# Folding a long convolution's transforms by reflection, and summing a gated unit in the output by DMA

## The chip, the core and the metric

The kernel runs on one core of a Trainium2 chip. The core has five engines that work side by side, each through its own queue in order: TensorE (PE; its weight loads are shown as PEld), VectorE (DVE), ScalarE (ACT), GpSimd (POOL) and SyncE (SP). Data comes and goes by 16 DMA engines, whose transfers are issued from SP's and POOL's queues. PE writes its results to PSUM (eight banks of 128 partitions by 512 float32 each), from where DVE or ACT move them to SBUF.

The metric is the time on the device in microseconds (us). Lower is better.

## What is computed

The input `x` is 2048 rows of 512 channels. Two results are mixed by a gate of each row:

```python
g = sigmoid((x * gate_w).sum(-1, keepdims=True))
# a: a long convolution of each channel; its kernel comes from 128 complex states
K[d, l] = real(sum_n C[d, n] * exp(dt[d] * A[d, n] * l) * dt[d] * B[d, n])
a = irfft(rfft(pad(x.T)) * rfft(pad(K)))[..., :2048].T + x * Dskip
# b: a gated unit, 512 -> 1792 -> 512
b = (sigmoid(x @ w_gate) * (x @ w_up)) @ w_down
out = g * a + (1 - g) * b
```

All inputs and the output are float32.

## The kernel before

**Dense work (b).** The rows are taken in two halves of 1024, each in two blocks of 512 columns (`sb`); the 1792 hidden channels in 14 slices of 128. Each operand of a dense product is split into a high part that PE's fast float32 mode takes whole and a low rest (ACT copies the high part, line 884; DVE subtracts, 885), and a product is three matmuls. `hidden` (938) makes one slice of gate and up for one block: four turns of PE of six matmuls (line 953). `post` (991) applies the sigmoid, multiplies and splits the result. `down` (1013) multiplies with `w_down` in groups of 3, 4, 4 and 3 slices, three matmuls per turn (1030). `add` (1040) scales a group's sum by 1 - g: the first group goes to an accumulator in SBUF (1046), the next ones through a staging tile `part` (1053) and an accumulating DMA from POOL into it (1055); for the second half's last group DVE adds from PSUM (1066). The first half's sums go out to a DRAM tile `acc0` (1060). The split weights of the first half's 14 slices are stored in DRAM (`wsp`, from `keep`, 932) and loaded again for the second half (913 and the next function).

**The convolution's kernel (a).** Channels come in 16 groups of 32. For each group `bases` (408) makes angles, sines, cosines and powers; `tables` (491) builds a table T of 32 steps by five doublings (`double`, lines 459 to 461, DVE), `magnitudes` (465) a table B of 64 (ACT's exponentials, DVE's products, 471 to 486). One batch of 128 small matmuls, `kps` (527), multiplies T with B to the group's kernel of 2048 samples. `first` (536) sorts it (541), adds Dskip, does the first step of its transform (`wps`, 555) and brings it out (`kev`, 565) to a DRAM tile `a_k`.

**The transforms.** The long transform is done in two steps with DRAM between them. `rows` (581) loads 16 tiles of 128 rows of x, takes the dot product with `gate_w` (591) and does u's first step (`ups`, 606), stored in `a_u`. `passes` (633) then works on two halves of the channels (j = 0, 1; 256 each), each in eight parts p: `ustep` (677; `s2u`, 690) is u's second step, `kstep` (702; `s2k`, 715) the kernel's, with the complex product on DVE (726 to 733); `inverse` (738; `ips`, 761) is the first step back, brought out by `evict` (769) to `b_s`. When all eight parts are there, `finals` (795) loads `b_s` again and `last` (810) does the last step (`fps`, 819) and adds g times it to the sums (828 for the first half, which is loaded from and stored to DRAM, 835 for the second).

**The order.** Every generator above yields its steps with the engine that runs them. The order of all steps is written out by hand in the string ORDER: each letter names a kind and an engine ("hidden PE", "tables DVE", "add POOL"), one turn each, and `Plan.run` (202) takes the steps in that order. So the sequence on each engine's queue is fixed by ORDER, and the turns ahead of any step can be counted in it; a turn is one step as it is yielded, which may hold several instructions. "-" turns only take buffers. The PSUM banks are three for `hidden`, one for `down` (joined with the others at the end), four for the rest.

Matmuls come in tile modes: dense work uses the whole 128x128 array, the batches use it as several smaller arrays side by side: kps 128x32 (rows by columns), wps and ips 32x64, ups 64x128, s2u and s2k 64x32, fps 128x64.

Of the kernel before, what the change touches and what calls it, by code (L numbers as in the profile page):

```python
# [32 lines left out]
L, D, F, NS = 2048, 512, 1792, 128  # L33
# [6 lines left out]
ANGLES = list(range(33)) + [64 << k for k in range(5)]  # L40
NA = len(ANGLES)
POWERS = list(range(1, 64, 2)) + ANGLES[33:]
NP = len(POWERS)
# [3 lines left out]
WIDTHS = [256, 256]  # L47
BANKS = dict(gu=3, dn=1, xb=4)
# [3 lines left out]
TURNS = ("ustep PE", "ustep ACT", "ustep DVE", "ustep -", "inv PE", "inv ACT", "inv DVE", "inv SP", "inv -", "x SP", "w SP",  # L52
         "split ACT", "split DVE", "rows PE", "rows ACT", "rows DVE", "rows SP", "rows -", "dn SP", "urest ACT", "urest DVE",
         "urest SP", "bases ACT", "bases DVE", "bases -", "tables PE", "tables DVE", "tables -", "first PE", "first ACT", "first DVE",
         "first SP", "first -", "mags ACT", "mags DVE", "hidden PE", "post ACT", "post DVE", "down PE", "add ACT", "add DVE",
         "add SP", "add POOL", "passes SP", "step PE", "step DVE", "step -", "finals SP", "last PE", "last DVE", "last SP", "last -",
         "const SP", "steps DVE", "steps SP", "preludes ACT", "preludes DVE", "preludes SP", "pw SP", "splitw ACT", "splitw DVE",
         "splitw SP", "splitd ACT", "splitd DVE", "splitd SP")
ORDER = (
    "211JLMK78jJLK7MJLK8jjMj1j07JLMjjK78jjJLSkKj2K!8jjJJ77#lkL8jjMlkmS!L55MS#!8jjJ643M4X0RLMkXYlWXjjkjjkWQPOjllRNWlkmlWj#9UKW"  # L60
    "jKmXj78TWaikaanR7hahaaa$Ql9maaPiiiikmjlKSXXam7ORNRQP0$TjjnVjmVmK75!Tjkm8akYjWXlOnRNWjmjTkjljUkamWm0jal9aRQaWP8ORN#RQPnaV"
    "blVUOZ9WXKTRNV8WaiaaaaVKkRjaaQmaadeTVhmhTmaPlijnkig7Vj7iiORcdmjddmNKRlXXkmTYjKjQTPjWaaXnVmkjjOaaV7WRkmlWlWW5mNaa8lnk8XWT"
    "b8Zla$ijV7Taa8kjaajjjaalaaRQPhhjimiidORN$de9miaKXaS!a9#VkljmKVTTSgSjXn!VcY#jWX7dkkjdmjR7KjkmVladdQPORjNRWQPOlfaWakabZlU8"
    "RWlNWjX!#VWdaik8jlTjahmahmnaaj43eTmkm7mmg0ajajiTjaiicRinmmKQP8ORq7ljk4madmXjdXYWk$jjdadVnqlmmaXWNRQPkOWaWm8aaaVTmWqan9lX"
    "KTW7VbZRNlVaidTT9ahjh$qaaKaakmmaajm8jegRQPkajikiiOmna7ciXmaqXdmVdm5majYWXanVmmmaRlldWaWVajmWlqKb8WjX7kNWUlZ9aijja8kVajK7"
    "ajaRnQaaqhjhljka9Paadmmk8dK7m$mnORNRTQijljjiiilS!Xj#Sk5XSYWTkPK!ejX!7l#Tmmaja#amWaf9jklalgcORjabWS!WklK#VVkdjZWdlm7XWdNK"
    "djdnmmm8qjmRaihhqTTkaaaaeQagcdnjmm7mmd8qaajdPiiiiXXaYW$nqj89K7jOakXWWWWaamRmaamamalVlNnXW8bZaKkkih$am8jjjmlm43qamaVhT4ji"
    "iTaadfni7mmmmkjinmmmmaXaaXYqW8jXdenWagaacjqamjqJSaalkdjabm5W!#SWWlX!#ldZVj$mLjWJVkakmdddiheVghScaaanlLajkldMj9admjimJidj"
    "jkiiaX!#dmjXYaaW$XnamjmLWJqW9mljanmWaaWKVaLjkaabMZMXfrrrrrrkqdllmmMeWaKpnJai5DABBusrrtktrJgalatjhjjammlJhicddddqijatjraI"
    "EjqakrkimFaJilFDFKFXLlHnXABMBusYkjWttXLmtatLmWrrajlrkaWajIjMHEFFrrrmjnmmW$WLmDABarBaGGHqSpuabHsplnprrXkZWtmlmamiajkardeg"  # L70
    "ttljcMnMmmhhratIraajadSiiaid$jddEFiFamDrFAFBXHBustHtXYkWtaqtjkXrjInajjEaGljkqWFWrFalFlrDABWrkrmaBaabmjustSlWXfmnrZWmtmjm"
    "jdHaihtj4eKaarqg3tkancr4mamhiiadiIdaiadaXmnjkrlKjrmaHdEFrFFFKaXmYaDmnHHAlWkBBaXuWsrajarrlabmjkpWWtlrmttjmrnkZtplrjWXjdIE"
    "rGDmWaipFaeFFaHHABBusrrrrrtjatahtathiii$mimjkaagncajXjdammdXYIddEFFFFaKDmWjkqaXSABHpBusljrjtjaHWtttInmmkEaaGabjkWfFljFFW"
    "ZWXlWjkSaiajdajHaheghlaamcaHvladjkkiajvdvzwyivzwyiSvvlxjyxldidkaXyXjkYzyjlnmmvaWXSjaWjjklWaWjaWjxaabvlXmZwyyzxKyklvvWaai"
    "wyjvjykldhxmnjmzhiimmmaxikqvniyXljmazakwwmxmxxxyaXjYmyWaXvjyvxnmamxWekammgncWmaldWaaajdaWmzaamXjdbwldZxWKxmnjjdmkmmaiham"
    "KaaafhaajneamgacdKaakamivqjaidddmviajmizawabxZnmmdxSSllekgcdddjdjfrrrrljkljkljkjjjjmkjlrjrDrlrrrrkACBuKsttttklDjrjlqkrjq"
    "SArBrBustjmjnmljktqSktrtIErrrrrrFFGrGGlmqjDlFklFmHFjjmqqHnACBursrrDrmrmtttmmntqACCHuHstjjtmtmtIKmmnrEGDmrrFrrrFFHrDmmmrj"
    "kljFFKACCuFFHsrjnrkmHtrlmmyttABBtustttmjktnmIjmEFjmGFHDFFqFGmnrABrGCuslrkttmttrrmrmrrmnDjHHABCustmtHtrjtHmmljqSIEklFFGjk"
    "mGSjGjkGGjSFlyHnmmlklmjjkqjomHHmlHmovvzvvwyzwyxvjjvzyxmjmyvyvzvmjyvzkwywkxqyvvzvwlxxxjqyyvyzljyjmkvlmvmzykmmxylxwxkwwylm"
    "mmxoxoqxyypxoqxmopmmpxpmommxmoypp")  # L80

XLATE = 0
SLACK = dict(dma=1.6, eng=0.06)
FETCH = 6.5


def constants():
# [7 lines left out]
    wf = fwd.reshape(P, 64) / L  # L95
    wk = np.tile(fwd.reshape(P, 2, 32).transpose(2, 1, 0).reshape(32, 2 * P), (4, 1))
    l2, k2 = np.arange(32)[:, None], np.arange(32)[None, :]
    wwu = np.zeros((8, 2, 32, 2, 4, 2, 32))
    wwv = np.zeros((8, 4, 32, 2, 2, 32, 2))
    for p in range(8):  # L100
        for r in range(2):
# [1040 lines left out]
```

## Time and profile before

| | |
|---|---|
| runs | 619.85, 624.1 and 628.68 us, median 624.1 us |
| profiled execution | span of 621.9 us, from the first instruction to the last; it is one execution, and no time of its own beside the span is recorded |
| busy | PE 609.1, DVE 518.1, ACT 426.5, POOL 35.1 us |
| granted clock of TensorE | 0.997 of full on the mean |
| DMA | 140.35 MB, mean 226 GB/s |
| instructions | 16371 |

The profile is one execution. A row of a group of instructions has the line in the kernel, the engine, the operation, the tiles written and read, the shapes, the count, then busy time in us and the mean length of one in ns, and last the idle time of the engine ahead of them with what ended it. Lengths of successive instructions overlap a little. A row of the timeline has start, length, engine, line and count. A chain row is a stretch of the chain of work that ended last, followed back from the end. SPq is SP's queue of DMA issues.

### The profile page before, as it was taken

To read this page: it belongs to the slowest core of one execution; us is meant where nothing else is said; L and a number is where in the kernel's file an instruction comes from. 1 tells how busy PE (TensorE), PEld (TensorE's weight loads), DVE (VectorE), ACT (ScalarE), POOL (GpSimd) and SP (SyncE) were. 2 spreads that over 40 slices of the span, in tenths; PEclk is the share of its full clock that TensorE was granted. 3 is DMA by queue.
4 is the path that set the end of the run, shared out by engine and by line. 5 is a ranking of instruction groups with operands and counts; after the bars stand their busy time and mean duration, and the time that the engine had idled before them with its cause. 6 is when DMAs were issued, how large, how long until landed. Compare 5 with 4: busy or idle time off the path is not lost.

```text
span 621.9 us, 16371 instructions
## 1 busy us (share of the span) xinstructions
PE 609.1 (98%) x6816; PEld 462.3 (74%) x6816; DVE 518.1 (83%) x927; ACT 426.5 (69%) x705; POOL 35.1 (6%) x44
## 2 busy tenths in 40 slices
PE   6999999999999999999999999999999999999997
PEld 4877777777778777877767777777787777667775
DVE  5879999998999999999999999997996276438334
ACT  6698897979899988998878787768585221322110
POOL 0000000011110101010100000000110001100000
PEclk9999999999999999999999999999999999989999
DMA  6964775594595729899999869666775989999784
GB/s 220 373 220 131 218 270 172 172 292 115 175 358 177 203 36 298 293 295 271 200 289 288 245 154 274 197 192 223 224 207 155 253 206 240 236 269 257 212 269 146
DMA packets 97162, 140.35 MB, mean 226 GB/s; under 512 B 40000, under 2 KB 65472, under 8 KB 92480
## 3 DMA queue, kind: packets, MB, share of 16 engines
q1 hardware_dynamic: 91328, 128.81, 67.7%
q0 software_dynamic: 5760, 10.49, 10.2%
q8 instruction: 54, 0.88, 0.6%
q14 instruction: 20, 0.16, 0.1%
HBM read 75.31 MB, written 53.48 MB: 207 GB/s over the span
## 4 chain that ended last, share of the span: by engine, by line
PE 84%; DVE 6%; DMA 4%; ACT 4%; issue 1%; SPq 1%; DVEq 0%
PE gups L953 44%; PE dps L1030 22%; PE kps L527 4%; PE ups L606 3%; PE wps L555 3%; PE fps L819 2%; PE ips L761 2%; PE s2u L690 2%; PE s2k L715 2%; DMA ak<-a_k 1%; DMA gu<-wsp 1%; DMA a_k<-kev 1%; DVE T L460 1%; DMA st<-wgu 1%; DVE uf L727 1%
## 5 line engine op out<-in xcount | busy, mean ns | idle before, releaser
L953 PE MATMUL gups<-x,gu 128*128 128x512 f32 x1344 | 334.0, 396 | 6.1 <-ACT gu L884 6.1
L953 PEld LDWEIGHTS gups<-x,gu 128*128 128x128 f32 x1344 | 251.0, 189 | 74.2 <-issue 13.4
L1030 PE MATMUL dps<-dnw,h 128*128 128x512 f32 x672 | 177.2, 397 | 0.3 <-issue 0.3
L1030 PEld LDWEIGHTS dps<-dnw,h 128*128 128x128 f32 x672 | 123.8, 188 | 36.2 <-issue 9.2
L1055 POOL DMA_DIRECT2D acc<-part x40 | 34.9, 873 | 542.4 <-ACT part L1053 510.9
L1001 ACT ACTIVATE h<-sg 128x512 fp32r<-128x512 f32 x56 | 34.7, 627 | 30.5 <-DVE sg L997 30.3
L477 ACT ACTIVATE B<-B 128x32 f32<-128x32 f32 (+2 forms) x96 | 53.3, 668 | 0.4
L997 DVE TENSOR_TENSOR sg<-gups,sg 128x512 f32<-128x512 f32 x56 | 38.2, 685 | 17.6 <-PE gups L953 13.3
L1053 ACT ACTIVATE part<-dps,omg 128x512 f32<-128x512 f32 x40 | 27.4, 686 | 31.1 <-PE dps L1030 30.8
L461 DVE TENSOR_TENSOR T<-T,t 128x64 f32<-128x64 f32 (+4 forms) x80 | 46.5, 582 | 1.3
L459 DVE TENSOR_TENSOR t<-T,bz 128x64 f32<-128x64 f32 (+4 forms) x80 | 46.2, 577 | 1.1
L460 DVE TENSOR_TENSOR T<-T,bz 128x64 f32<-128x64 f32 (+4 forms) x80 | 46.3, 579 | 0.0
L995 ACT ACTIVATE sg<-gups 128x512 f32<-128x512 f32 x56 | 33.4, 596 | 15.2 <-PE gups L953 15.0
L1002 DVE TENSOR_TENSOR h<-sg,h 128x512 fp32r<-128x512 f32 x56 | 38.2, 686 | 5.7 <-ACT h L1001 5.7
L565 ACT ACTIVATE kev<-wps 128x256 f32<-128x256 f32 x64 | 34.7, 643 | 7.0 <-PE wps L555 6.9
L527 PEld LDWEIGHTS kps<-B,T 128*32 128x32 f32 x2048 | 29.3, 110 | 8.3 <-issue 4.5
L527 PE MATMUL kps<-B,T 128*32 128x64 f32 x2048 | 31.9, 220 | 0.5 <-DVE T L461 0.5
L297 ACT ACTIVATE ev<-ips 128x256 f32<-128x256 f32 x47 | 14.6, 390 | 25.5 <-PE ips L761 25.5
L297 ACT ACTIVATE uf<-s2u 128x512 f32<-128x512 f32 x24 | 13.4, 596 | 24.1 <-PE s2u L690 23.9
L726 DVE TENSOR_TENSOR tt<-s2k,uf 128x512 f32<-128x512 f32 x32 | 22.0, 686 | 4.1 <-PE s2k L715 3.9
L434 ACT ACTIVATE af<-ex 128x1216 f32<-128x1216 f32 x16 | 19.6, 1222 | 7.5 <-DVE ex L431 7.5
L995 ACT ACT_TABLE_LOAD x19 | 24.4, 1283 | 0.3
(87 smaller groups left out, 700.5 us busy)
## 6 DMA issues: line engine op xcount, KB each, us to landing
wsp<-gu SPq DMA_DIRECT2D x14, 1024.0 KB, 6.6
gu<-wsp SPq DMA_DIRECT2D x14, 1024.0 KB, 7.4
acc<-part POOLq DMA_DIRECT2D x40, 256.0 KB, 5.9
a_u<-evu SPq DMA_DIRECT2D x32, 256.0 KB, 4.9
a_k<-kev SPq DMA_DIRECT2D x8, 1024.0 KB, 5.6
au<-a_u SPq DMA_DIRECT2D x32, 256.0 KB, 5.3
ak<-a_k SPq DMA_DIRECT2D x32, 256.0 KB, 6.8
b_s<-ev SPq DMA_DIRECT2D x32, 256.0 KB, 4.4
```

The source lines that it names most:

```text
L459: yield "DVE", dve(n), lambda: V.tensor_tensor(t2, src, sb, op=OP.mult), [t, slot.t]
L460: t = yield "DVE", dve(n), lambda: V.tensor_tensor(dst, src, br, op=OP.mult), [t]
L461: t = yield "DVE", dve(n), lambda: V.tensor_tensor(dst, dst, t2[:, :, ::-1], op=OP.add), [t]
L477: A.activation(B[:, :, 0, 1 << k::2 << k], B[:, :, 0, 1:64 >> k:2], AF.Exp, scale=float(1 << k))
L527: mm(p[32 * jj:32 * jj + 32, s], T[:, ch, c], B[:, ch, c], start=(c == 0), stop=(c == 1), tile_position=(0, 32 * jj), skip_group_check=True)
L565: te = yield "ACT", 0.475, lambda: A.activation(kev[:, :, o:o + 2].rearrange("p k s -> p s k"), ph[jj], AF.Copy), [t, kv.t]
L953: mm(p, gu[:, a, k, dc], x[:, b, dc], start=(dc + n == 0), stop=(dc == NC - 1 and n == 2))
L995: t = yield "ACT", ("sig", act(512)), lambda: A.activation(sg, pg_, AF.Sigmoid), [tg, ss.t]
L997: t = yield "DVE", dve(512), lambda: V.tensor_tensor(sg, pu, sg, op=OP.mult), [t, tu]
L1002: t = yield "DVE", dve(512), lambda: V.tensor_tensor(h[:, 1], sg, h[:, 0].bitcast(F32), op=OP.subtract), [t]
L1030: mm(p, h[:, a, 128 * s:128 * s + 128], dn[:, b], start=(f == f0 and n == 0), stop=(f == f0 + gn - 1 and n == 2))
L1055: ts = yield "POOL", kb(430), lambda: nc.gpsimd.dma_start(accs[t], part, accum_op=OP.add), [te, begun[t]]
```

## The change

- **Folding.** The rows of x are laid out so that each sample stands across from its mirror images. `rows` works on four blocks of four tiles: DVE forms sums and differences of mirrored tiles (two folds of two instructions with 1024 elements each), and u's first step needs then half of the products: 8 batches `ups` of 16 matmuls in 32x32 tiles instead of 16 batches. `ustep` does two parts p at once in 8 batches of 32 matmuls in 32x32 tiles; `inverse` likewise; `last` makes folded sums for four tiles at once (8 batches), which DVE unfolds (four instructions of 512), ACT scales by g.
- **Sums in the output.** There are no accumulators in SBUF any more, and no `acc0`. The first group's scaled sum is written to the output by SP; all others, and the convolution's part (`last`), are added to the output in DRAM by accumulating DMAs from POOL: 48 of 256 KB and 32 of 128 KB instead of 40 of 256 KB into SBUF.
- **Second half in reverse.** The second half takes the slices of the hidden channels from the last to the first; the last three slices' split weights stay in SBUF, and 11 instead of 14 are stored and loaded again.
- **Tables by pairs.** T is built for 64 channels at once (the last doubling in two parts); angles stay per group (32 instead of 38 of them), the powers are made per pair of groups. `wps` takes two groups per batch and is brought out by two ACT instructions of 1024 elements instead of eight of 256.
- **Banks.** The four banks of the batches become two pairs; `kps` takes `down`'s bank.
- **Order.** ORDER is written anew for these steps.

```diff
-ANGLES = list(range(33)) + [64 << k for k in range(5)]
+ANGLES = [b + 0.5 for b in range(32)]
+SCALES = [31.5] + [64 << k for k in range(5)]
-BANKS = dict(gu=3, dn=1, xb=4)
+BANKS = dict(gu=3, dn=1, xb=2)
...
+    XB = slots(ps, "xb", BANKS["xb"], [P, 2, 512])
...
+    def double(T, b, e, parts, t):
+        nd = 64 // parts
+        n = 2 * nd * e
+        for i in range(parts):
...
+            yield "DVE", dve(n), lambda: V.tensor_tensor(t2, src, sb, op=OP.mult), [t, slot.t]
+            te = yield "DVE", dve(n), lambda: V.tensor_tensor(dst, src, br, op=OP.mult), [t]
+            te = yield "DVE", dve(n), lambda: V.tensor_tensor(dst, dst, t2[:, :, ::-1], op=OP.add), [te]
...
+                t = yield from double(T, bz[:, :, k], e, max(1, e // 8), t)
...
+                bank, = yield DNS, 1
+                p = bank.tile("kps", [P, 8, 64])
...
+            def fold(a, b):
+                V.tensor_tensor(a, a, b, op=OP.add)
+                V.scalar_tensor_tensor(b, b, -2.0, a, op0=OP.mult, op1=OP.add)
+            t = yield "DVE", 2 * dve(1024) + 0.2, lambda: fold(u[:, 0], u[:, 1]), tu
+            t = yield "DVE", 2 * dve(1024) + 0.2, lambda: fold(u[:, :, 0], u[:, :, 1]), [t]
...
+                                mm(ph[jj // 2][o:o + 32, jj % 2], wu[rr, c, r], u[rr, c, e], start=True, stop=True,
+                                   tile_position=(32 * jj, o), skip_group_check=True)
...
+                            mm(pu[s][32 * g_:32 * g_ + 32, r, i], wwu[q, i, g_], au[i][q, g_], start=True, stop=True,
+                               tile_position=(64 * s + 32 * r, 32 * g_), skip_group_check=True)
...
+                            mm(pi[g_ // 2][o:o + 32, g_ % 2, i], wwv[q, i, r], uf[q, i, r, c], start=True, stop=True,
+                               tile_position=(32 * g_, o), skip_group_check=True)
...
+        def sums():
+            V.tensor_tensor(mn[:, 0], ph[:, 0], yt, op=OP.add)
+            V.tensor_tensor(mn[:, 1], ph[:, 0], yt, op=OP.subtract)
...
+                t1.append((yield "ACT", act(W) + 0.1, lambda: A.activation(y[:, i], y[:, i], AF.Copy, scale=g[:, t:t + 1]), [te]))
...
+                done.append((yield "POOL", kb(215), lambda: nc.gpsimd.dma_start(out[t, :, cols], y[:, i], accum_op=OP.add), [max(t1), begun[t]]))
...
-        ("sg", 3, [P, 512], F32), ("hs", 8, [P, 2, 512], F32R), ("acc", 8, [P, D], F32)))
+        ("sg", 3, [P, 512], F32), ("hs", 8, [P, 2, 512], F32R)))
...
+    KEEP = GROUPS[-1]
+    SLICES = [list(range(NF)), list(range(NF - 1, -1, -1))]
...
+        te = yield "ACT", act(512) + 0.1, lambda: A.activation(part, p, AF.Copy, scale=omg[:, t:t + 1]), [tp, gate[t, 1].t, ss.t]
+        bank.free(te)
+        if gi == 0:
+            ts = yield "SP", kb(256), lambda: S.dma_start(out[t], part), [te]
+        else:
+            ts = yield "POOL", kb(430), lambda: nc.gpsimd.dma_start(out[t], part, accum_op=OP.add), [te, begun[t]]
```

More of the change, by code (lines that the diff above doesn't have):

```diff
@@ L612, in urest @@
+    def urest(t4, e, i, ph, banks, tp):
         es, = yield EVU, 1
         ev = es.tile("evu")
[L614 to L621 removed]
@@ L685, in mms, with kstep @@
+    def kstep(i, wks, wwk, sk, ak, ready, both, tk):
+        yield ready[0]
+        ufs, uf = ready[1]
+        yield near(tk)
+        bank, = yield XB, 1
+        pk = bank.tile("s2k", [P, 2, 2, W])
         def mms():
@@ L693, in ustep @@
-        sa.free(t)
-        tu = 0.0
-        for r in range(2):
-            te = yield ("ACT", "DVE"), {"ACT": act(2 * w), "DVE": dve(2 * w)}, lambda eng: copy(eng, uf[:, r], pu[r]), [t, ufs.t]
-            banks[r].free(te)
-            tu = max(tu, te)
-        ready[1] = ufs, uf, tu
-        ready[0].set(tu)
-    def kstep(j, wus, wwu, sk, ak, ready, both, tk):
-        w = WIDTHS[j]
-        yield ready[0]
-        ufs, uf, tu = ready[1]
-        yield near(tk)
+        t = yield "PE", ("64x32", 0.92, 66), mms, [tk, bank.t]
```

1009 lines of the change are left out of this document (517 added, 492 removed).

## The prediction

> **What bounds the kernel now.** I read the page's first part and its chain of waits, then the busy time of the engines in five stretches (cut at the eleventh and the last table batch), then single rows.
>
> ```profile
> PE 609.1 (98%) x6816; PEld 462.3 (74%) x6816; DVE 518.1 (83%) x927; ACT 426.5 (69%) x705; POOL 35.1 (6%) x44
> ...
> PE 84%; DVE 6%; DMA 4%; ACT 4%; issue 1%; SPq 1%; DVEq 0%
> ```
>
> TensorE is busy nearly all the time and carries 84% of the chain. Read alone, that says: whatever is taken off PE is gained. The stretches say more (columns: length, busy time of PE, PEld, DVE, ACT, POOL, each with its instructions, granted clock, DMA share, GB/s):
>
> ```profile
> 0.00:40.00 40.00, 33.89 (x136) 26.30 (x137) 28.56 (x71) 27.54 (x42) 0.20 (x4) 1.00 0.77 266
> 40.00:340.00 300.00, 299.51 (x3442) 227.41 (x3441) 289.26 (x499) 267.34 (x439) 21.00 (x24) 1.00 0.77 225
> 340.00:474.00 134.00, 133.53 (x1768) 102.24 (x1767) 124.70 (x221) 98.57 (x158) 5.20 (x6) 1.00 0.71 211
> 474.00:560.00 86.00, 84.30 (x1086) 62.74 (x1084) 43.67 (x80) 23.71 (x50) 6.64 (x8) 0.98 0.98 237
> 560.00:622.00 62.00, 57.86 (x399) 43.65 (x390) 31.86 (x59) 9.31 (x18) 2.08 (x3) 1.00 0.74 221
> ```
>
> Up to the last table batch (474) there are two full engines: PE, and VectorE with 442.5 of 474 us. Only behind it is DVE half idle, and there DMA is full for 86 us (0.98). The eleventh table batch shows how the two meet:
>
> ```profile
> 338.60 1.22 DVE L461 TENSOR_TENSOR T<-T,t 128x1024 f32<-128x1024 f32 x1
> ...
> 339.99 1.21 PE L527 MATMUL kps<-B,T 128*32 128x64 f32 x72
> ```
>
> DVE's last table product ends at 339.82, and PE starts the batch 0.17 us later. Both queues are in order and written out in ORDER, so a new order can be judged at each table turn by two sums: the PE work ahead of it, and the DVE work that its table needs.
>
> **What the change takes off PE.** The prices of PE's work (start and length of runs on the chain; then rows of the timeline, where a batch is charged from its start to that of the next row):
>
> ```profile
> 39.52 1.36 PE dps L1030 x6
> ...
> 64.51 1.92 PE kps L527 x128
> ...
> 106.18 1.14 PE wps L555 x63
> ...
> 508.52 1.91 PE ips L761 x64
> ...
> 587.98 1.88 PE fps L819 x16
> ```
> ```profile
> 323.30 1.09 PE L690 MATMUL s2u<-au,wwu 64*32 64x256 f32 x32
> 324.19 1.67 PE L715 MATMUL s2k<-ak,wwu 64*32 64x256 f32 x32
> ...
> 331.46 1.12 PE L761 MATMUL ips<-uf,wwv 32*64 32x256 f32 x32
> 332.51 1.66 PE L953 MATMUL gups<-x,gu 128*128 128x512 f32 x6
> ...
> 338.07 1.09 PE L715 MATMUL s2k<-ak,wwu 64*32 64x256 f32 x32
> 339.10 0.96 PE L1030 MATMUL dps<-dnw,h 128*128 128x512 f32 x3
> ```
> ```profile
> 32.71 1.13 PE L606 MATMUL ups<-u,wu 64*128 64x512 f32 x4
> 33.77 0.96 PE L1030 MATMUL dps<-dnw,h 128*128 128x512 f32 x3
> ```
>
> A hidden turn (6 dense matmuls) is 1.36, a down turn (3) 0.68; s2u 0.89 (s2k follows it in the same tile mode), s2k 1.03, ips 1.05 (a double one 1.91), ups 1.06, fps 0.94 (two in 1.88), kps 1.92, wps 1.14. Dense work and kps stay. Folding halves the batches of ups, s2u and fps (16 each to 8 each) and brings ips from eight single and four double ones to 8; wps pairs its batches (16 to 8 double ones). The new batches of ups, s2u and ips use 32x32 tiles, which no row shows. Between the nearest rows: 16 tiles that run together need what a half-sized grid needs for half the work, 1.0; if only eight ran together, 1.91, as the double ips. I take 1.05, nearest to ips, which already uses four row strips; wps double 2.05, fps 1.0. Saved: ups 17.0-8.4 = 8.6, s2u 14.2-8.4 = 5.8, ips 16.0-8.4 = 7.6, fps 15.0-8.0 = 7.0, wps 18.2-16.4 = 1.8: 30.8 us. Changes of tile mode (adjacent PE turns of different mode in ORDER) fall from 158 to 133, some 0.1 each (s2k, followed by another mode, costs 0.14 more than s2u): 2.5. So PE's queue, start of 6.1, turns times prices and changes, shrinks from 606.6 (its measured end is 617.9, below) to 573.2.
>
> **What it does to DVE.** The rows that price it, by form:
>
> ```profile
> L421 DVE TENSOR_TENSOR ex<-pp,pw 128x1216 f32<-128x1216 f32 x16 | 22.7, 1419 | 0.1
> ...
> L486 DVE TENSOR_TENSOR B<-B,ex 128x1024 f32<-128x1024 f32 x16 | 19.5, 1219 | 0.0
> ...
> L443 DVE TENSOR_TENSOR bz<-ex,ep 128x320 f32<-128x320 f32 x16 | 12.5, 783 | 7.0 <-ACT ep L438 6.8
> ...
> L459 DVE TENSOR_TENSOR t<-T,bz 128x512 f32<-128x512 f32 x16 | 11.0, 687 | 0.1
> ...
> L541 ACT ACTIVATE kst<-kps 128x512 f32<-128x512 f32 x16 | 9.5, 593 | 2.3 <-PE kps L527 2.3
> ...
> L459 DVE TENSOR_TENSOR t<-T,bz 128x256 f32<-128x256 f32 x16 | 6.7, 421 | 0.2
> ...
> L423 DVE TENSOR_TENSOR ep<-pp,pw 128x160 f32<-128x160 f32 x16 | 5.1, 318 | 0.0
> ...
> L459 DVE TENSOR_TENSOR t<-T,bz 128x128 f32<-128x128 f32 x16 | 4.7, 291 | 0.3
> ```
> ```profile
> 254.54 0.69 DVE L1002 TENSOR_TENSOR h<-sg,h 128x512 fp32r<-128x512 f32 x1
> 255.14 0.29 DVE L459 TENSOR_TENSOR t<-T,bz 128x128 f32<-128x128 f32 x1
> ```
>
> Back to back, an instruction costs some 0.085 us less than its row (0.60 between starts for 0.69). So 1024 elements cost 1.135, 512 cost 0.60, 256 cost 0.335. Ahead of the eleventh table turn, old order against new, counted along ORDER:
>
> Folds of u: 16 instructions of 1024, new, +18.2. Products of the passes: nine pairs of 512 and eight of 256 (16.3) against two pairs of 1024 and two of 512 (6.9), -9.4. Tables: 11 groups of 8.05 (15 products and a start) against 6 pairs of 14.35 (18 products and a start), -2.5; pairing saves the fixed part of the small products but the sixth pair must be whole. Angles: 12 groups of 3.60 against 24 products of 1.135 and 6 power sets; the set's 640-element product lies between 0.78 (if the 320-element row is all layout) and 1.57 (twice it), I take 1.4, together 43.2 against 43.1. Hidden results: 65 against 59 of 0.60, -3.6. Evictions and small ones -1.0. Sum +1.6: the folding adds on DVE what the merging saves. DVE was busy 28.56 + 289.26 = 317.8 by then, 12.9 of it stalls between dependent instructions (the same count of rows gives 305); with 451 instead of 554 instructions the stalls lose 2.4. So **DVE needs 317 busy us before the eleventh table, as it did.**
>
> PE's sum ahead of the same turn falls from 334.9 (measured 340.0) to 292.5: 129 hidden and 100 down turns instead of 137 and 115 (the first eight of the hidden ones are half turns), 28 batches instead of 50, 52 mode changes instead of 83. PE will stand and wait for the table. Behind it PE has 280.7: 99 hidden turns 134.6, 124 down turns 84.3, 14 kstep 14.4, six tables 11.5, last 8.0, inv 7.4, ustep 6.3, three second 6.2, changes 8.1. (The old order had 271.7.) Without any stall, DVE's need is 4 to 16 us above PE's sum at every table (308 against 292.5 here, 422 against 418.8 at the last); in the old order it was 12 to 43 below (305 against 334.9, 425 against 467.7).
>
> The Trainium skill says, in "TensorEngine Tiling (Array Packing)", Performance Considerations (PSUM Bottleneck), that tiling speeds TensorE but not the emptying of PSUM, which may become the bound. By that rule PE's saving need not be the time's saving; the trace has DVE full in the same way (289 of 300 us), though more with tables than with emptying.
>
> **The sum.** DVE was idle 11.4 us in the first 40 and 10.7 in the next 300. With PE waiting for DVE, idle time is bounded by 2 (the first load) and 22 (as before); the new order feeds folds and dots of u to DVE in the first 40 us, so I take 9. Table at 317 + 9 = 326. Then 280.7. Later waits were 617.9 - 340.0 - 271.7 = 6.2; bounds 0 and 8, I take 2, since fewer weight reloads meet the full DMA. The end:
>
> ```profile
> 615.65 2.20 PE L1030 MATMUL dps<-dnw,h 128*128 128x512 f32 x9
> ...
> 617.89 0.75 DVE L1066 SCALAR_TENSOR_TENSOR acc<-dps,omg,acc 128x512 f32<-128x512 f32 x1 [0.90 <-PE dps L1030]
> ```
> ```profile
> acc<-part POOLq DMA_DIRECT2D x40, 256.0 KB, 5.9
> ...
> out<-acc SPq DMA_DIRECT2D x8, 256.0 KB, 2.2
> ```
>
> PE ended at 617.9, and DVE's 0.75 and a store of 2.2 brought 621.9. Now the tail is an ACT scaling and an accumulating DMA of 5.9 instead of 2.2: 4.0 + 3.7, and up to three issues queued ahead on POOL, 7 to 11; I take 7. Sum 326 + 280.7 + 2 + 7 = 616 for the span. The median of the runs (624.1) stands 2.2 above the profiled span (621.9), which gives **618**.
>
> At nothing I cost: ACT (ahead of that turn 6% less work by the same count; the merged kev evictions replace the old ones); the weights of three slices that stay in SBUF instead of going out and back (13.6 MB with the sums' store and reload; PE stood still for 1 us in all between 40 and 474, at DMA shares of 0.77 and 0.71); the sums' own traffic (24 more accumulations' worth against the loads saved); SP's issues. Behind 474 DVE gets 28 us of sums of folded rows, but was idle 72.5 of 148 there. If DMA's relief counts, it takes the later waits to 0; if not, they are 6 to 8. Two waits are new on PE. kps now shares the single bank of down, which is free again after ACT's 0.593 copy; behind every table turn ORDER has a hidden turn or another batch (1.03 or more) before the next down turn, so nothing; without that cover 16 x 0.7 = 11. And a batch of ups, s2u, ips or wps now takes both bank pairs, each emptied by a copy of 1024 (1.2); 63 of the 72 batches follow dense work, the other nine could stand 1.1 each, 10 in all, at least 0; 1 of my 2 us is for that.
>
> **Rivals.** (1) PE stays the bound: 573.2 + 11.3 (measured minus counted, 617.9 - 606.6) + 7 = 592, on the runs 594. For it: 98% and 84%. Against: it needs the eleventh table at 298 (292.5 and the old order's 5.1 of waits), while DVE has 317 busy us of work before; the count would have to be 20 us too high. (2) The accumulating queue at the end: rows 8 to 15 get their last group and their second final sum within PE's last 30 us, all on POOL in order, and each second one must wait until the first has landed (5.9); behind it stand the other accumulations, with them the staging tiles that ACT's scaling needs (six instead of eight), and so PSUM banks. If all eight pairs wait in full, 47 us stand in 30, with other issues behind them, and the last landings come 17 to 20 late: 638, slower. It decides where a pair lies closer than 6 us; in ORDER two pairs do (3 to 5 us of PE work apart), the others are 7 to 10 apart, so I give it little. "DMA: Bandwidth & Descriptors", Rules for kernel authors, in the Trainium skill demands that wait for any accumulation beside another access of the same bytes; no run here shows an accumulation in DRAM. (3) 32x32 tiles run only eight at a time: 0.9 more for each of 24 batches; those ahead of the eleventh table hide in PE's wait, the 13 behind add 12: 630.
>
> **Chances.** Forecast 0.66 (own range 605 to 634: idle 2 to 22, waits 0 to 8, tail 7 to 11, not all at an end), (1) 0.14, (2) 0.12, (3) 0.05, others 0.03. A change of 2% (to 611.6 or 636.6) is about what can be told from none. Faster: (1), a quarter of the forecast, and half of the others: 0.32. Slower: half of (2) and a twelfth of the forecast, with scraps: 0.13. Within: 0.55. The range 600 to 637 leaves out (1) and the far part of (2).
>
> **What would show it.** PE's busy share falls from 98% to about 93 to 95%, with waits of the table batches (kps) for DVE's T or B growing from 0.5 us in all to 20 or more, nearly all up to the eleventh table; DVE stays near 97% up to the eleventh table; dense matmuls keep 1.36 for six; a 32x32 batch takes 1.0 to 1.1; the span ends 6 or 7 us behind PE's last matmul. I am wrong if the eleventh table starts before 315 (DVE's count too high), if PE idles behind it for more than 10 us (DMA or PSUM slots), or if POOL's waits reach the end.

## The result, and the profile after

| | before | changed |
|---|---|---|
| median of the runs | 623.8 us (619.85 to 628.68, 4 runs) | 657.3 us (653.4 to 659.1, 4 runs) |
| ratio | | 1.053, 95% interval 1.047 to 1.059 |
| profiled span | 621.9 us | 655.8 us |
| start of the eleventh table batch | 340.0 | 334.2 (predicted 326) |
| start of the last table batch | 474.1 | 463.8 |
| PE's last matmul ends | 617.9 | 644.4 |

The changed kernel is slower by 5%; the prediction (618, range 600 to 637) was wrong, and on the wrong side of no change. Up to the last table it is 10 us ahead, and the stage behind it is 44 us longer (192.0 us instead of 147.8). Some of the 44 was planned: counted along ORDER, PE's own work behind the last table grew from 139 to 154 us (534 dense matmuls instead of 450), and by the sum of the forecast that stage should have taken 163 us. So 28 to 29 us of it are lost. Two of the four executions of e3 (676.4 and 678.7 us) and of e4 (659.9 and 660.0) took over 1.5% longer than the fastest of their kernel; times and ratios below leave them out, but the only profile of e4 is of the one of 660.0. The page of the changed kernel: busy times, the granted clock and the DMA share in 40 slices, the chain of waits by engine.

```profile
PE 599.2 (91%) x7136; PEld 454.4 (69%) x7136; DVE 518.2 (79%) x726; ACT 444.3 (68%) x668; POOL 70.3 (11%) x84
...
PEclk9799989999999999997999999999899989999997
DMA  7585581668828686964389469186599999999988
...
PE 45%; DVE 17%; issue 12%; DMA 11%; ACT 6%; SPq 4%; POOL 4%; POOLq 0%; DVEq 0%; ACTq 0%
```

PE carried 84% of the chain and now carries 45%; no engine has taken its place, the rest is spread over DVE, DMA, waits and issues. The last 11 slices of the DMA row lie behind the last table: nothing but nines and eights. The stretches, cut at the eleventh and the last table batch (columns as in the prediction: length, busy time of PE, PEld, DVE, ACT, POOL, granted clock, DMA share, GB/s):

```profile
0.00:40.00 40.00, 28.36 (x149) 18.68 (x149) 32.63 (x79) 23.68 (x41) 0.20 (x4) 0.91 0.73 236
40.00:334.20 294.20, 275.37 (x3337) 216.09 (x3340) 285.50 (x389) 256.65 (x376) 17.55 (x20) 0.98 0.64 184
334.20:463.80 129.60, 128.47 (x1846) 99.88 (x1844) 119.36 (x153) 104.14 (x150) 5.21 (x6) 1.00 0.69 193
463.80:560.00 96.20, 86.77 (x1102) 62.56 (x1109) 45.19 (x60) 29.57 (x50) 17.87 (x21) 0.95 1.00 244
560.00:620.00 60.00, 56.75 (x572) 39.97 (x566) 25.58 (x34) 19.47 (x35) 11.11 (x13) 1.00 1.08 267
620.00:656.00 36.00, 23.49 (x154) 17.27 (x152) 9.97 (x15) 10.76 (x20) 18.36 (x21) 0.89 0.89 120
```

Up to the eleventh table DVE was busy 32.63 + 285.50 = 318.1 us, and idle for 16. Behind the last table DVE and ACT are idle for more than half of the time (busy 80.7 and 59.8 of 192), PE is not full either (167.0 of 192), and the DMA share is 0.9 to 1.1 to the end. Single rows of its timeline, by stage:

```profile
27.17 1.14 PE L661 MATMUL ups<-u,wu 32*32 32x512 f32 x32
28.24 8.45 PE L1040 MATMUL gups<-x,gu 128*128 128x512 f32 x36
...
334.16 1.04 PE L577 MATMUL kps<-B,T 128*32 128x64 f32 x60
...
366.77 1.49 PE L823 MATMUL ips<-uf,wwv 32*32 32x256 f32 x64
368.20 3.01 PE L1040 MATMUL gups<-x,gu 128*128 128x512 f32 x12
...
377.94 1.49 PE L761 MATMUL s2u<-au,wwu 32*32 32x256 f32 x64
379.36 4.37 PE L1040 MATMUL gups<-x,gu 128*128 128x512 f32 x18
...
463.78 1.88 PE L577 MATMUL kps<-B,T 128*32 128x64 f32 x119
469.62 0.33 PE L577 MATMUL kps<-B,T 128*32 128x64 f32 x9 [3.97 <-issue]
...
637.55 6.87 PE L1110 MATMUL dps<-dnw,h 128*128 128x512 f32 x29 [0.23 <-DVE h L1088]
...
649.31 0.87 POOL L1129 DMA_DIRECT2D out<-part  x1 [0.42 <-issue]
```

A batch of ups takes 1.07 as predicted, but ips and s2u take 1.43 and 1.42 instead of 1.05 (the trace has two instructions for each of the program's matmuls in these batches, 32 for ups and 64 for the others). The last table batch stands still in its middle for 3.97 us. Behind PE's end POOL still issues accumulations up to 649.3 and the last ones land near the span's end.

The forecast span was 616; measured 655.8. By the steps of its sum: the eleventh table 334.2 instead of 326, +8.2; from there to PE's end 310.2 instead of 280.7 + 2, +27.5 (3.4 of it ahead of the last table); the tail 11.4 instead of 7, +4.4.

What PE waited for up to the eleventh table, and then what DVE, ACT and PE waited for behind the last one (time in all, times, longest):

```profile
PE kps L577 <- DVE B L515: 8.1, 3, 3.3
PE gups L1040 <- ACT gu L946: 6.3, 1, 6.3
PE gups L1040 <- DVE x L947: 4.6, 2, 2.3
PE gups L1040 <- ACT sg L1081: 3.8, 3, 1.9
```
```profile
DVE ev L309 <- DMA out<-mn: 9.2, 1, 9.2
...
ACT ev L309 <- DMA out<-mn: 6.1, 2, 4.1
...
DVE yt L309 <- DMA out<-yt: 4.6, 1, 4.6
...
PE s2k L788 <- DVE ev L309: 3.2, 1, 3.2
```

The 6.3 us are the start, which the kernel before has too (6.1). For the rest of the front ACT stands among PE's releasers as often as DVE, seven times each, for 9.1 us against 14.0. Behind, the evictions of `ips` (tile `ev`) and the unfolding (`yt`) stand for accumulations of the final sums (`mn`, `yt`) to land: those tiles share two tags with the passes and are held until POOL's accumulating DMA is done. PE then waits for the evictions. And the DMA queues behind the last table, before and after (packets, MB, the packets' time as a share of 16 engines over that stage of 147.8 and 192.0 us; q0 is POOL's queue, q1 SP's):

```profile
q1 hardware_dynamic: 34256, 31.20, 76.3%
q0 software_dynamic: 1440, 2.62, 11.0%
```
```profile
q1 hardware_dynamic: 35480, 33.59, 64.4%
q0 software_dynamic: 7776, 9.96, 35.2%
```

In time: 112.8 + 16.3 = 129 of 147.8 us before, 123.6 + 67.6 = 191 of 192.0 after. SP's queue moved about as much as before; the accumulations went from 2.6 to 10.0 MB, and a MB of them took 6.8 us, where SP's took 3.7. This gave three theories for the 28 us (of the 40) that are lost behind the last table, the tail with them. *Order*: accumulations into the same row wait for each other, in POOL's order. *Slots*: tiles held until an accumulation lands. *Traffic*: the DMA engines are full, and the accumulations are what fills them. And one for the front: *ring*, DVE and ACT bound it together.

### The profile page after: what moved, and what is told of

Read it like the earlier page. It is cut to its first block, busy times and chain, and to the rows that moved or that the text cites. A ratio compares the mean times of both kernels' runs of the same rounds, so it can differ in the third digit from the quotient of the medians.

```text
span 655.8 us, 16738 instructions
## 1 busy us (share of the span) xinstructions
PE 599.2 (91%) x7136; PEld 454.4 (69%) x7136; DVE 518.2 (79%) x726; ACT 444.3 (68%) x668; POOL 70.3 (11%) x84
## 3 DMA queue, kind: packets, MB, share of 16 engines
HBM read 67.97 MB, written 63.44 MB: 200 GB/s over the span
## 4 chain that ended last, share of the span: by engine, by line
PE 45%; DVE 17%; issue 12%; DMA 11%; ACT 6%; SPq 4%; POOL 4%; POOLq 0%; DVEq 0%; ACTq 0%
PE gups L1040 23%; PE dps L1110 11%; PE kps L577 4%; POOL out L905 3%; PE wps L607 2%; PE s2k L788 2%; DMA out<-mn 2%; DMA u<-xp 2%; DMA ak<-a_k 1%; DMA out<-part 1%; DMA out<-yt 1%; DVE t L533 1%; DVE sg L1083 1%; DVE T L535 1%; DVE T L534 1%
## 5 line engine op out<-in xcount | busy, mean ns | idle before, releaser
L1129 POOL DMA_DIRECT2D out<-part x48 | 42.6, 888 | 482.9 <-ACT part L1124 337.3
L1124 ACT ACTIVATE part<-dps,omg 128x512 f32<-128x512 f32 x64 | 43.6, 681 | 63.7 <-PE dps L1110 60.9
L1087 ACT ACTIVATE h<-sg 128x512 fp32r<-128x512 f32 x56 | 34.9, 626 | 16.5 <-DVE sg L1083 16.2
L533 DVE TENSOR_TENSOR t<-T,bz 128x1024 f32<-128x1024 f32 (+3 forms) x48 | 41.3, 861 | 1.5 <-ACT ez L436 0.9
L535 DVE TENSOR_TENSOR T<-T,t 128x1024 f32<-128x1024 f32 (+3 forms) x48 | 41.4, 863 | 0.2
L534 DVE TENSOR_TENSOR T<-T,bz 128x1024 f32<-128x1024 f32 (+3 forms) x48 | 41.5, 864 | 0.0
L616 ACT ACTIVATE kev<-wps 128x1024 f32<-128x1024 f32 x16 | 31.0, 2006 | 5.5 <-PE wps L607 5.5
L798 DVE TENSOR_TENSOR tt<-s2k,uf 128x1024 f32<-128x1024 f32 x16 | 19.6, 1225 | 18.4 <-PE s2k L788 18.3
L431 ACT ACTIVATE af<-ex 128x1024 int32<-128x1024 f32 x16 | 16.9, 1059 | 13.3 <-DVE ex L484 13.3
L788 PE MATMUL s2k<-ak,wwk 64*32 64x256 f32 x512 | 19.2, 397 | 5.7 <-DVE ev L309 3.2
L901 ACT ACTIVATE yt<-yt,g 128x256 f32<-128x256 f32 x16 | 7.4, 502 | 24.7 <-DVE yt L894 24.7
```

Source lines behind the costliest of these rows:

```text
L533: yield "DVE", dve(n), lambda: V.tensor_tensor(t2, src, sb, op=OP.mult), [t, slot.t]
L534: te = yield "DVE", dve(n), lambda: V.tensor_tensor(dst, src, br, op=OP.mult), [t]
L535: te = yield "DVE", dve(n), lambda: V.tensor_tensor(dst, dst, t2[:, :, ::-1], op=OP.add), [te]
L1087: t = yield "ACT", act(512), lambda: A.activation(h[:, 0], sg, AF.Copy), [t, hs.t]
L1124: te = yield "ACT", act(512) + 0.1, lambda: A.activation(part, p, AF.Copy, scale=omg[:, t:t + 1]), [tp, gate[t, 1].t, ss.t]
L1129: ts = yield "POOL", kb(430), lambda: nc.gpsimd.dma_start(out[t], part, accum_op=OP.add), [te, begun[t]]
```

## Experiments behind the last table

**Final sums as plain stores, final sums into their own rows, final sums from their own tiles.**

```diff
-nc.gpsimd.dma_start(out[t, :, cols], y[:, i], accum_op=OP.add)
+nc.gpsimd.dma_start(fsc[t, :, cols], y[:, i])                    # e1
+nc.gpsimd.dma_start(b_s[j][i, int(slot is es), 4 * t4:4 * t4 + 2]
+    .rearrange("j k d -> (j k) d"), y[:, i], accum_op=OP.add)    # e2
```
```diff
-        ts, = yield fin["t"], 1
-        es, = yield fin["ev"], 1
+        ts, = yield EZ, 1
+        es, = yield KST, 1                                       # e3
```

> The 32 final sums (128 KB each) go as plain stores to a scratch array instead of accumulating into the output rows; the convolution's part is left out of the output, every issue stays where it was on POOL. Three theories of the 27.5 us lost behind the eleventh table and of the 4.4 us in the tail. Order (an accumulation waits for the one before it in the same row, and POOL behind it): dense excess behind the last table goes from 16.6 back to some 6, the tail from 11.4 to about 8, so 657 - 11 - 3 = 643. Slots (the finals' tiles lie in the passes' two tags and are held until their accumulations land): the same place, but a plain store still holds them for a landing, so half of it: 650. Traffic (the DMA queues are full from 464 to 620, and an accumulation moves its bytes twice): 4.2 MB less at some 240 GB/s are 17 us: 640. None of these (batch prices, clock, code loading): 656.

> The 32 final sums still accumulate, with the same bytes, from the same tiles, in the same place of POOL's queue, but into rows of the scratch array that fed them, which nothing else touches by then; the convolution's part is left out of the output. Order: no wait for an earlier accumulation of the row, so as without accumulation, 643 (657 - 14). Slots: tiles are held for one landing instead of a wait and a landing, 650. Traffic: nothing is saved, 657.

> Nothing is left out: the finals' two tiles move from the tags that they share with the passes (t, ev) to two tiles of the tables that are free by then (ez, kst), one each. Order: the same accumulations in the same order, 655. Slots: the evictions of ips and the products of s2k no longer wait for an accumulation's landing; of the gaps of PE behind the last table the two at 533 and 565 (3.3 and 2.3) and the dense excess of 16.6 shrink, 657 - 13 = 644. Traffic: 657.

Measured: e1 650.6 us (ratio to the kernel before 1.048, interval 1.043 to 1.054), e2 651.9 (1.050, 1.045 to 1.054), e3 669.7 (1.078, 1.068 to 1.088). Without the waits for the same row, and with all the traffic, e2 is 5 us faster than the changed kernel by the medians, but by the ratios the two can't be told apart (1.050 and 1.053, with overlapping intervals); taking the accumulation out of the final sums (e1) adds hardly anything to that. None of the three gives the 13 to 17 us that its theory promised. e3 went the other way by 12, with a stage behind the last table of 210.4 instead of 192.0, and its timeline says how:

```profile
496.17 0.69 DVE L309 COPY yt<-fps 128x512 f32<-128x512 f32 x1 [9.50 <-DMA out<-yt]
...
502.31 0.69 DVE L888 TENSOR_TENSOR mn<-fps,yt 128x512 f32<-128x512 f32 x1 [5.45 <-DMA out<-mn]
502.92 0.68 DVE L889 TENSOR_TENSOR mn<-fps,yt 128x512 f32<-128x512 f32 x1
...
503.70 2.33 PE L761 MATMUL s2u<-au,wwu 32*32 32x256 f32 x60 [7.71 <-issue]
```

With one own tile each (in the changed kernel behind the last table they have two, shared), every set of final sums waits for the last set's accumulation to land; DVE stands 9.5 and 5.5 us with its queue behind it; the bank of `fps` stays full, and PE stands 7.7 us for it in the middle of a batch (the profile calls that "issue", since the wait is for a bank that DVE gives back at 503.6). So held tiles are a real cost, but the way to lower it is more tiles:

**More tiles.** Behind the last table the two tables of 16 KB are cut up (order of all engines unchanged):

```diff
-                for n, s in (("big", TB[0]), ("big", KEV[0]), ("big", EX[0]), ("uf", TA[0]), ("ev", T2[0]), ("t", T2[1]), ...
+                for src, names in ((TB, ("mn", "mn", "mn", "yt", "yt")), (TA, ("uf", "mn", "yt", "yt")),
+                                   (KEV, ("big", "big")), (EX, ("big", "big"))):
```

> Nothing is left out: behind the last table the two 16 KB tables are cut into pieces, so that the finals have four pairs of tiles of their own and the passes one more load tile than now; order of all engines unchanged. Slots: no eviction and no bank waits for an accumulation's landing: with one own pair instead of shared ones the time rose by 18, with four it falls to what the own rows gave or lower, 645 to 650. Traffic: within 3 of 657. Order (same row): POOL's waits stay, 655.

Measured: 655.0 us, ratio 1.051 (1.044 to 1.059), which cannot be told from the changed kernel's 1.053. The waits of PE for evictions are gone, and others stand in their place:

```profile
PE fps L898 <- DMA b_in<-b_s: 3.6, 4, 1.5
PE s2u L783 <- DMA au<-a_u: 2.2, 1, 2.2
```

The waits have moved from landings of accumulations to landings of loads. That speaks for traffic, which the next three kernels change directly.

**All accumulations plain; and, the other way, more traffic.**

```diff
-nc.gpsimd.dma_start(out[t], part, accum_op=OP.add)
+nc.gpsimd.dma_start(gsc[gi - 1, t], part)          # e5, with the stores of e1
```
```diff
-lambda: S.dma_start(b[q][64 * c:64 * c + 64], src)
+lambda: (S.dma_start(b[q][64 * c:64 * c + 64], src), S.dma_start(xsc[...], src))   # e6; e12 likewise
```

> All accumulations (the 48 group sums of 256 KB and the 32 final sums of 128 KB) go as plain stores to scratch arrays; the output keeps the first group's part alone. Behind the last table the changed kernel moved 33.5 MB on the hardware queue (64.2% of 192 us, 3.7 us per MB) and 10.0 MB of accumulations (35.2%, 6.8 us per MB): 191 of 192 us, against 128 of 148 us in the kernel before. With the final sums plain, the same queue took some 49 us for the same bytes, so a plain store costs some 2.3 us per MB. Traffic (the stage is bound by the DMA engines): 123 + 23 = 146 us, less than PE's 154 of work, so PE bounds again: 464 + 154 + 4 of waits + 8 of tail + 2 = 632. Order and slots alone (what the final sums' stores already took away): 648.

> Nothing is left out; each of the 32 loads of b_in is followed by a copy of the same 256 KB to a scratch array in DRAM that nobody reads or waits for: 8.4 MB more behind the last table. Traffic: 8.4 x 3.7 = 31 us more, 688. Order and slots (waits for landings, engines not full): SP's 32 more issues of some 0.6 are spread over 140 us; 657 to 662.

> The kernel before, nothing left out, with the same addition as the changed kernel got: behind each of the 32 loads of b_in a copy of its 256 KB to a scratch array in DRAM that nobody reads. There it cost 15.4 us for 8.4 MB behind the last table. In the kernel before 16 of the 32 loads lie between the eleventh and the last table, where DMA was at 0.71, and 16 behind it, where the packets took 128 of 148 us. Slack: the first 16 cost nothing, the other 4.2 MB take some 14 us of the 20 that are free: 622 to 627. No slack (a DMA share of 0.98 from 474 to 560 is as full as the changed kernel's): half of 15.4 or more, 631.

Measured: e5 639.2 us (1.0255, 1.020 to 1.031), 18 faster than the changed kernel; e6 672.2 (1.077, 1.072 to 1.083), 15 slower; e12 632.6 (1.011, 1.005 to 1.018), 8 slower than the kernel before. The same two rows of the queues, for the stage behind the last table, of e5 (175.4 us), e6 (204.9) and e12 (154.0):

```profile
q1 hardware_dynamic: 35426, 33.29, 73.0%
q0 software_dynamic: 3296, 9.96, 15.2%
```
```profile
q1 hardware_dynamic: 44191, 42.01, 69.7%
q0 software_dynamic: 7776, 9.96, 33.5%
```
```profile
q1 hardware_dynamic: 38608, 35.40, 81.2%
q0 software_dynamic: 1440, 2.62, 10.2%
```

The same 9.96 MB take 26.7 us as plain stores (15.2% of 175.4) and 67.6 as accumulations: 2.7 against 6.8 us per MB. Traffic gave the direction of e5 and e6 and too much of both (25 and 31): 36 us of packets' time less made the stage 17 shorter, 20 more made it 13 longer, so a us of packets is worth about half a us, as an estimate. In time, e5 lies halfway between traffic (632) and order with slots (648), and e6 halfway between 688 and 657 to 662. Neither changes bytes alone: e5 also takes away the group sums' waits for their row and shortens POOL's issues behind the last table from 50.5 to 29.3 us, and e6's copies are 32 more issues on SP's queue, 28 us of issuing; these parts weren't separated. e12, with 16 more issues (8 us) there, shows that the price held in the kernel before too, as "no slack" (631) had it: 4.2 MB more behind its last table made that stage 6.2 us longer (and the other 4.2 MB, ahead of it, 3.5), although its packets filled only 129 of 148 us.

**Row sums in SBUF.** A version that leaves nothing out: rows 8 to 15 are summed in the place of the last T table and go to the output once. (`put`, whose main line is the third one shown, adds to a row; the other tables are cut into more load tiles than before, much as in e7.)

```diff
+        whole, = yield TA, 1
+        acc = whole.tile("acc", [P, 8, D])
...
+            V.scalar_tensor_tensor(row[:, cols], src, sc[:, t:t + 1], row[:, cols], op0=OP.mult, op1=OP.add)
...
+            nc.gpsimd.dma_start(out[t], rows_[t][0], accum_op=OP.add)
...
+            te = yield "ACT", act(512) + 0.1, lambda: put(t, None, p, omg), [tp, gate[t, 1].t]
```

> Nothing is left out: behind the last table the sums of rows 8 to 15 are taken in SBUF (in the place of the last T table, 8 rows of 2 KB, by VectorE or ScalarE at the place where ScalarE's scaling was), and each row is accumulated into the output once, at its end; the accumulations behind the last table fall from 10.0 MB to some 4.7 MB. Traffic: 5.3 x 6.8 = 36 us of DMA time less, 155 of 192, about PE's own 154 of work: as with plain stores, 638 to 643. If it is not the traffic but what accumulating waits for (same rows, POOL in order): the last rows still wait for a landing at the end, 648.

Measured: 647.0 us (1.038, 1.034 to 1.042), 10 faster than the changed kernel. Traffic at its full price (638 to 643) promised more; the 648 of the other theory is met, but so is half a us for each of the 24 us of packets saved: the stage is 10 us shorter. So this run doesn't tell the two apart. Its queues in the stage of 182.4 us:

```profile
q1 hardware_dynamic: 35475, 33.57, 73.8%
q0 software_dynamic: 3600, 4.46, 18.1%
```

The accumulations fell from 67.6 to 33.0 us, and SP's packets took 11 us longer. Put together, the stage behind the last table of all kernels but e4 (shares times length, from the queues' rows; SP's + POOL's queue):

| kernel | MB | packets' time, us | stage, us |
|---|---|---|---|
| before | 34.1 | 113 + 16 = 129 | 147.8 |
| before, loads twice (e12) | 38.3 | 125 + 16 = 141 | 154.0 |
| all plain, less work in front (e11, below) | 43.5 | 130 + 27 = 157 | 174.8 |
| all plain (e5) | 43.5 | 128 + 27 = 155 | 175.4 |
| row sums (e10) | 38.3 | 135 + 33 = 168 | 182.4 |
| final sums plain (e1) | 43.8 | 132 + 49 = 181 | 185.8 |
| own rows (e2) | 43.9 | 127 + 68 = 195 | 187.2 |
| less ScalarE (e9, below) | 43.9 | 126 + 67 = 193 | 190.1 |
| no folds, less ScalarE (e8, below) | 43.9 | 127 + 69 = 196 | 190.7 |
| more tiles (e7) | 43.9 | 130 + 68 = 197 | 190.7 |
| changed | 43.8 | 124 + 68 = 191 | 192.0 |
| loads twice (e6) | 52.2 | 143 + 69 = 211 | 204.9 |
| own tiles (e3) | 43.8 | 127 + 69 = 196 | 210.4 |

With one exception the length of the changed kernel's stage goes up with the packets' time, if not in every pair: over 155 to 211 us of packets, 175 to 205 us of stage. Some of the scatter is a stall of PE in the last table batch or soon behind it (last section): 3.6 to 4.4 us in the profiles of the changed kernel, e1, e3, e5, e10 and e11, some 1.3 in the others with the new order. So of the 4.8 us by which e2's stage is shorter than the changed kernel's, about 3 are the stall, and what the waits within rows cost is 2 us or nothing. Slots (e7) and an earlier front (e8) change the stage by 2 us at most; e3 alone is off the line, where the tiles became the bound. In the plain kernels PE ends 170 us behind the start of the last table, still 16 above its own work (154, counted along ORDER at the prediction's prices).

## Experiments in front

**No folds; less ScalarE; both.** The folds act on 16 columns instead of 1024 (e4, e8); the sigmoid becomes a copy and the angles' sines act on 1 of 32 rows (e8, e9).

```diff
-            t = yield "DVE", ..., lambda: fold(u[:, 0], u[:, 1]), tu
+            t = yield "DVE", ..., lambda: fold(u[:, 0, 0, :16], u[:, 1, 0, :16]), tu
...
-        A.activation(sg, pg_, AF.Sigmoid)
+        A.activation(sg, pg_, AF.Copy)
-        A.activation(f, f, AF.Sin, scale=-2 * math.pi)
+        A.activation(f[:, :1], f[:, :1], AF.Sin, scale=-2 * math.pi)
```

> DVE's 16 folds of u (1.135 each, 18.2 in all) act on 16 columns instead of 1024, so the transform gets unfolded rows; all else stays. If DVE bounds up to the eleventh table, that table starts near 334 - 17 = 317 and the whole ends 17 earlier if the work behind it does not meet a full DMA, 640; if the stage behind the last table is paced by DMA and its waits, part of it is lost there, 645 to 652. If DVE was not the bound (PE's own work and waits were), the eleventh table stays within 3 us of 334 and the time at 656.

> As the kernel without folds, and ScalarE relieved too: the hidden layer's sigmoid is a copy (13 fewer loads of a function table of 1.28 by the eleventh table, and the loads that follow them) and the sines of the angles act on 1 of 32 rows (11.5 + 3.1); so the hidden layer's activation and the tables are not those of the reference. Without folds alone the eleventh table stayed at 331 (331 to 335 in all runs so far), and the chain to it went from DVE 78, ACT 28 to DVE 43, ACT 65. If DVE and ACT bound the front together, the eleventh table now starts at 318 or earlier (PE's sum of 292.5 + some 20 of starting and local waits), and the time follows by 10 or more unless the rear takes it back. If it is something else (PE itself, DMA), it stays above 326.

> ScalarE relieved as in the run before (the sigmoid a copy, the sines on 1 of 32 rows), but with the folds in full; the activation and the tables are not those of the reference. The eleventh table stood at 331 to 335 with both loads, at 331 without the folds, at 323 without either. Ring (DVE and ACT wait for each other in turn, and each alone is close to full): 327 to 331, less than the 8 to 11 of both; the rear keeps its length of some 190, so 652 to 655. If ScalarE alone set the front: 323 and 644.

Measured: e4 ratio 1.041 (1.035 to 1.047); e8 643.6 us (1.032, 1.026 to 1.038); e9 653.9 (1.048, 1.041 to 1.055). The eleventh table, one row of each timeline, of e4, e9 and e8:

```profile
330.83 0.88 PE L577 MATMUL kps<-B,T 128*32 128x64 f32 x48
```
```profile
331.21 0.99 PE L577 MATMUL kps<-B,T 128*32 128x64 f32 x56
```
```profile
322.74 0.98 PE L577 MATMUL kps<-B,T 128*32 128x64 f32 x54
```

In eight profiles with the front unchanged it starts between 331.3 and 335.3. The stretch from 40 us to the eleventh table, in the same order (columns as above; the changed kernel's row has 285.50 for DVE and 256.65 for ACT):

```profile
40.00:330.80 290.80, 272.37 (x3320) 213.93 (x3318) 270.88 (x383) 252.23 (x371) 17.54 (x20) 0.98 0.62 182
```
```profile
40.00:331.20 291.20, 273.75 (x3333) 215.81 (x3333) 284.62 (x388) 233.76 (x364) 17.54 (x20) 0.98 0.64 186
```
```profile
40.00:322.70 282.70, 269.06 (x3322) 211.48 (x3320) 271.09 (x383) 230.57 (x360) 17.57 (x20) 0.99 0.65 188
```

With the first 40 us, e4 takes 16.5 us off DVE's busy time and e9 22.8 off ACT's; either one moves the table by no more than that scatter, both together by 9 to 13. In e4 DVE's idle time up to the table rose from 16 to 29 us; with ACT relieved as well it was 20. So ACT alone does not set the front (323 by that theory, 331.2 in e9), and the rows speak for the ring: by DVE alone, e4 should have had the table at 317. But the ring is argued more than shown. What speaks against DVE alone is e4's one profile. The executions that its ratio stands for took 646.7 and 647.0 us, 10 less than the changed kernel; they fit "645 to 652", which was the case of DVE as the bound with a part lost behind the last table, and the interval of e4's ratio overlaps that of e8. Where these 10 us lie no profile shows. And e8's table came at 322.7, later than the 318 that the ring gave. The other side of e8 is in the table above: with the front 11 us earlier, the stage behind the last table kept its length, 190.7 us.

**All three reliefs together.**

> No folds, less ScalarE, and all accumulations as plain stores: the three reliefs together, the output is not the reference's. If front and rear are two limits one behind the other, the gains add: 657 - 13.5 (front) - 18 (rear) = 626. If the rear's loads are what holds it even then, the earlier front only runs into full queues: 632 to 637.

Measured: 627.7 us (1.007, 1.005 to 1.009), with the eleventh table at 322.5 and 174.8 us behind the last. The gains of front and rear add, to within 2 us of the sum: the two limits lie one behind the other. Together they are nearly the whole distance to the kernel before, though e11 also leaves out the sigmoids and most of the sines, which the kernel before computes. No version that computes everything was found that beats the kernel before; the best is the row sums, at 1.038.

## Why the prediction was wrong

- **PE's count.** It was nearly right: dense turns keep 1.36 for six, ups 1.07; PE's busy share is 91% where I gave 93 to 95, since the span is longer. Mis-sized: a batch of s2u or ips, 1.42 instead of 1.05 (bounds 1.0 to 1.91), since 64 instructions of 256 columns take 22 ns each and not the half of an instruction with 512 (33 ns in ups). 13 such batches behind the eleventh table cost 4.8 us more.
- **DVE up to the eleventh table.** "DVE needs 317 busy us" was right to a us (318.1). The step that failed is the idle time beside it: 9, measured 16, within its bounds of 2 and 22. The reading behind it is in doubt too: the rows speak for a ring of DVE with ACT, which I had put at nothing because its work shrank by 6%, though it was 84% busy (280.3 of 334.2). That DVE alone was the bound isn't excluded, as said above, so the cause of these 7 us stays open. The waits went another way than I said: of some 30 us in which PE waited up to that table, 6 were the start, 10 stood at table turns (20 or more was my sign) and the rest at dense turns, mostly behind ACT's and DVE's splitting and sigmoids.
- **"At nothing I cost ... the sums' own traffic".** This is the step that turned the sign. Its argument was that PE stood still for 1 us between 40 and 474, at DMA shares of 0.77 and 0.71. But most of the new accumulations lie behind 474, where the very rows that I had quoted say 0.98. There they went from 2.6 to 10.0 MB at 6.8 us per MB, 51 us more of packets' time; e5 took 41 of them away and gave 18 us back. At half a us each, an estimate from e5, e6 and e12, the 51 us are some 25 of the 28 that were lost there. I also took it that the weights kept in SBUF would relieve that stage; but SP's queue moved 33.6 MB there, against 31.2 before, so the relief lies elsewhere. "Later waits 2 (bounds 0 to 8)" stood on this: measured, with the dearer batches, 29.5.
- **The tail.** 11.4 instead of 7 (7 to 11). The last sums were still issued on POOL at 649.3; with plain stores (e5) the tail is 4.9. The mechanism was right, the size was just above its upper bound.
- **Rivals.** (1) fell: PE did not stay the bound. (2) named the right queue and the wrong mechanism: waits of POOL reach the end, as it said, but the price is not the order within rows in the last 30 us (e2 takes the final sums' waits away, for 5 us by the medians and 2 or less without the stall); what it missed is the accumulations' packets' time, over 190 us. (3) fell for ups; for s2u and ips 0.37 of the 0.9 that it feared came true. The Trainium skill, in "DMA: Bandwidth & Descriptors", Rules for kernel authors, asks for a wait for any accumulation beside another access of the same bytes; the kernel keeps that rule, and by e2 the waits cost little here, as said.
- **The median** stands 1.5 us above the profiled span (657.3 to 655.8), where the forecast took 2.2.
- **The range.** The forecast's own range of 605 to 634 does not follow from its bounds: with all of them at one end the sum gives 609 or 641, so 605 lies below what they allow.

What is left open: about 33 us of PE's dense time up to the eleventh table are above 0.227 per matmul even with both reliefs (e8), of which the first 40 us hold some 10; which waits of the ring make up the rest wasn't tried. Nor was it tried what sets the price of a 32x32 batch.

## What to carry to other kernels

Price an accumulating DMA by its packets' time, and charge it to the stage in which it lies: a mean DMA share, or the share of another stage, says nothing of the one that is full. And when two engines pass work to each other within a table or a batch, sum them both; in the profiles here relief of one alone moved the eleventh table by no more than its scatter, relief of both by 9 to 13 us.

## What was not expected of the hardware

- An accumulation's packets are shorter and slow. In the trace behind the last table, accumulating packets of 2 KB took 178 ns in the median and those of 1 KB 102 ns; the same stores without accumulation went in packets of 4 KB at 162 ns, and plain packets of 2 KB on SP's queue took 84 ns. Into SBUF (the kernel before) a 2 KB packet took the same 178 ns as into DRAM. So per byte an accumulation costs twice as much or more, wherever it goes. What the extra time is spent on the profile doesn't show: its count of bytes in DRAM is the same for the changed kernel and for e5 (67.97 MB read, 63.44 written).
- A stall in the middle of a batch, at one place of the program: with the changed kernel's order, the 5442nd matmul (in the last table batch, 463.78 and 469.62 above) started 3.6 to 4.4 us after the one before it in seven profiles; in the other five it was on time, and the 5569th, 127 matmuls on, started 1.3 us after the one before. The trace has a packet of 16 KB in a queue of instructions (q8) from 467.3 to 468.2, about 1.4 us ahead of the restart. That it is the fetch of instructions is argued from this, not shown; small batches take 128 matmuls in 2 us.
- PE's waits lower its clock. The kernel before had one interval at half clock between 11 and 620 us; the changed one has six up to PE's end, each 3.4 or 6.8 us long, 31 us in all (five of them are the sevens and eights of the clock's row ahead of its last slice). In the 3.4 us ahead of each of the six PE had stood idle for 2.0 to 2.9 us. Dense matmuls start 427 ns apart in them instead of 227, which costs the dense work some 6 us. The Trainium skill, in "TensorE: Matmul & The Clock Gate", Part 1, tells of a gate that halves the clock by windows of some 3.4 us without enough work; the trace agrees in the lengths. The same page of the Trainium skill, in Part 1, has a floor of about 25 ns between starts of small matmuls; here 128 of them in the kps batches take 1.92 us, 15 ns each, and the 32x32 batches 22, so that floor does not hold for matmuls that run side by side in tiles.
